# A new fixed order for the first batch of a packed-attention and two-MoE kernel, and keys by one transfer per four heads

## The chip, the cores and the metric

The kernel runs on one core of one Trainium2 chip. The metric is device time in microseconds (us) of one launch, the median of three runs. "PE" is TensorE, "DVE" VectorE, "ACT" ScalarE, "POOL" GpSimd and "SP" SyncE, whose queue starts nearly all transfers. A "product" below is one matmul instruction of the program; a product of plain fp32 operands shows as two MATMUL rows in the trace.

## The reference

```python
def sm_attn(qq, kk, vv):                      # per batch (8) and head (8); seq 576, head_dim 64
    s = scale * np.matmul(qq, kk.transpose(0, 1, 3, 2))
    s = s - np.max(s, axis=-1, keepdims=True)
    a = np.exp(s)
    a = a / (np.sum(a, axis=-1, keepdims=True) + 1e-09)
    return np.matmul(a, vv)
p_packed = sm_attn(p, k, v)                   # p: 32 packed queries per head
out = sm_attn(q, p_packed, p_packed)
x = out.transpose(0, 2, 1, 3).reshape(4608, 512)
x = gelu_like(x @ w_in) @ w_out               # w_in 512 x 2048, w_out 2048 x 512, given in float64
return (silu(x @ w_gate) * (x @ w_val)) @ w_out2
```

## The kernel before

**Two rounds.** Round one takes the eight batches in turn. Per batch it does the attention of two groups of four heads and the first MoE layer on the batch's 576 rows, in 32 units: two halves `t` of 288 rows, times 16 blocks `m` of 128 hidden columns. Round two does the gated layer; the change does not touch it.

**One unit.** `p1` (six products, tile `h`) multiplies `z`, the packed values already multiplied by `w_in`, with the second softmax `a2`. `tanh` (ACT) and `gate` (DVE, tile `g`) apply the activation. `hi` (ACT) and `lo` (POOL or DVE) split the result into a high and a low part, tile `gh`, so that three fast products stand for one of full precision. `p2` (twelve products, tile `acc`) multiplies by block `m` of `w_out`, tile `wo`. The tile `h` has two PSUM buffers, `gh` four.

**The attention of a batch**, per group `g`: `load_raw` brings keys or queries, `do_T` transposes them on DVE in two halves, `sc1` forms the scores of the packed queries (PE), `max1` (DVE), `exp1` (ACT) and `norm1` (DVE) make the first softmax. `a1T` transposes it on PE, `copy_a1T` copies it from PSUM, `pv` multiplies it with `v`. `do_D` copies 32x32 blocks of the result into `dz`; `do_F` (batch 0) or `do_E` and `split_E` (batch 1) put it into the form that `zm` multiplies with `w_in` (tile `zp`); `zh` and `zl` split that into `z`. `sc2`, `max2`, `exp2`, `norm2`, `ah` and `al` make the second softmax `a2`. All these take their PSUM buffers from one pool of two (`ps_a`).

**The weights in the first batch.** `w_in` and `w_out` arrive as float64 words. `stage` loads a block of 512 KB, `rebias` (ACT), `low` (ACT or DVE) and `join` (DVE) turn it into float32, `oh` and `ol` split a `w_out` block. `store_w n` writes two finished `w_in` blocks to DRAM (`win1`); in batch 1 `win`, `wch`, `wcl` and `wst` load, split and store them again (`win2`).

**What sets the order.** The string `FIRST` (line 19) is a list of these steps for batch 0, with the preparation of batch 1 marked by `+`. It is pinned: each engine gets its instructions in the order of the list, and each waits for what it needs. The list ends before `p1` of unit 32, the first of batch 1. From there on `STEADY` (line 79) holds, which the change leaves alone. Of the 32 units the list holds all `p1` and 29 `p2`, in both versions.

**Padding.** `warm n` (line 306) issues `n` products of a constant mask whose result nobody reads. The list of before holds twelve such steps, with 126 products.

**Keys.** `load_raw` (line 317) brings the queries of the first two batches with one transfer per group, in which each partition reads one run of 18 rows (4.6 KB). Keys come with four transfers, one per head, in runs of two rows:

```python
SP.dma_start(out=t[32 * h:32 * h + 32].rearrange("p (n r) d -> p n (r d)", r=2),
             in_=src[b, g * HG + h].rearrange("(n i r) d -> i n (r d)", i=32, r=2))
```

Of the kernel before, what the change touches and what calls it, by code (L numbers as in the profile page):

```python
# [20 lines left out]
    exp1 0; load_raw 1; warm 17; stage in 4; rebias in 4; do_T 1 0; do_T 1 1; stage in 1; pad_F 0; load_raw 2; do_T
    2 0; rebias in 0; sc1 1; warm 17; max1 1; low in 4 dve; join in 4; norm1 0; stage in 5; load_v 0 0; exp1 1;
    norm1 1; low in 0 act; stage in 7; rebias in 5; stage out 2; load_raw 3; a1T 0; copy_a1T 0; join in 0; pv 0;
    do_D 0 act; do_F 0; do_T 2 1; low in 7 dve; sc2 0 0; max2 0 0; low out 2 act; warm 9; rebias out 2; join out 2;
    do_T 3 0; rebias in 7; load_v 0 1; join in 7; a1T 1; copy_a1T 1; exp2 0 0; warm 5; stage in 6; low in 6 act; low
    in 5 dve; do_T 3 1; norm2 0 0; rebias in 6; pv 1; do_D 1 act; pad_F 1; do_F 1; warm 4; ah 0 0; stage out 0;
    stage out 13; join in 5; stage out 1; warm 6; low in 1 dve; stage in 3; oh 2; rebias in 1; al 0 0 dve; stage in
    9; join in 6; stage in 2; ol 2 pool; store_w 3; sc2 1 0; max2 1 0; exp2 1 0; low out 1 act; join in 1; zm 3; zm
    2; rebias out 0; store_w 2; norm2 1 0; rebias out 1; join out 1; ah 1 0; low out 0 act; al 1 0 pool; oh 1; ol 1
    pool; stage out 4; zh 3; zh 2; warm 27; zl 3 dve; zl 2 dve; store_w 0; join out 0; load_p 1; +do_p; low in 3  # L30
    dve; rebias out 4; zm 0; rebias in 3; rebias in 2; low in 2 dve; join in 2; join in 3; store_w 1; low out 13
    dve; zm 1; +p_ahead; zh 0; zl 0 dve; low out 4 act; p1 6; sc2 0 1; rebias out 13; stage in 8; rebias in 8; join
    out 4; zh 1; low in 8 dve; tanh 6; join out 13; stage out 8; zl 1 dve; p1 0; gate 6; rebias in 9; hi 6; stage in
    10; low in 9 act; stage in 11; stage out 5; tanh 0; rebias in 10; join in 8; max2 0 1; p1 2; tanh 2; warm 6;
    warm 5; gate 0; rebias in 11; join in 9; low in 11 dve; zm 4; lo 6 pool; oh 0; oh 13; sc2 1 1; p1 4; gate 2;
    join in 11; oh 4; stage in 15; low in 10 act; ol 0 dve; store_w 4; low out 5 act; exp2 0 1; ol 13 pool; ol 4
    pool; join in 10; max2 1 1; hi 0; lo 0 dve; low in 15 act; rebias in 15; hi 2; join in 15; zh 4; zl 4 dve; tanh
    4; rebias out 5; gate 4; zm 5; p1 1; lo 2 dve; join out 5; stage in 14; rebias in 14; zh 5; stage out 3; p1 3;
    p2 0; low out 3 dve; rebias out 3; join out 3; tanh 1; gate 1; stage out 10; hi 4; p1 5; zl 5 dve; low out 8
    act; lo 4 pool; rebias out 8; join out 8; stage in 13; p2 4; tanh 3; low in 14 dve; tanh 5; gate 3; oh 8; join  # L40
    in 14; zm 7; p1 8; stage in 12; low in 13 dve; rebias in 13; join in 13; rebias in 12; hi 1; lo 1 pool; low in
    12 dve; join in 12; zm 6; hi 3; stage out 12; load_raw 4; oh 5; ol 5 dve; p2 1; lo 3 dve; tanh 8; zh 7; oh 3;
    exp2 1 1; store_w 7; zh 6; zl 7 dve; low out 10 act; gate 8; rebias out 12; low out 12 act; hi 8; ol 3 pool; p2
    3; stage out 6; ol 8 pool; gate 5; hi 5; +do_T 0 0; +do_T 0 1; lo 8 pool; zl 6 dve; rebias out 10; stage out 9;
    p1 7; norm2 1 1; ah 1 1; al 1 1 pool; join out 10; low out 6 act; +sc1 0; +max1 0; p1 13; oh 10; ol 10 dve; tanh
    13; load_raw 5; +do_T 1 0; p2 8; +do_T 1 1; rebias out 6; load_v 1 0; tanh 7; join out 12; load_raw 6; join out
    6; +exp1 0; lo 5 pool; p2 5; +sc1 1; gate 13; oh 12; stage out 11; oh 6; gate 7; ol 12 pool; hi 13; low out 9
    act; store_w 6; +win 0; +max1 1; p1 11; +norm1 0; hi 7; p2 2; lo 13 dve; ol 6 pool; lo 7 pool; p2 6; +exp1 1;
    +norm1 1; store_w 5; rebias out 11; low out 11 act; join out 11; +a1T 0; wch 0; +copy_a1T 0; +do_T 2 0; +do_T 2
    1; oh 11; ol 11 pool; +win 2; tanh 11; stage out 7; gate 11; p1 10; tanh 10; wch 2; +pv 0; wcl 2 dve; p1 12; hi  # L50
    11; lo 11 dve; stage out 14; p2 13; +win 1; rebias out 9; gate 10; +do_D 0 act; +raw_ahead 0; wcl 0 pool; wst 0;
    rebias out 7; join out 9; hi 10; +do_E 0; low out 7 act; join out 7; lo 10 pool; +a1T 1; +split_E 0; p1 15; wch
    1; tanh 12; p2 11; +copy_a1T 1; +sc2 0 1; oh 7; wcl 1 pool; +zm 0 0; ol 7 dve; p2 7; gate 12; tanh 15; low out
    14 act; +win 4; gate 15; oh 9; +do_T 3 0; +zc 0 0; +max2 0 1; hi 15; lo 15 dve; p2 10; p1 14; +za 0 0; load_v 1
    1; tanh 14; p1 9; norm2 0 1; wch 4; ah 0 1; wcl 4 pool; +win 3; stage out 15; al 0 1 pool; gate 14; hi 14; tanh
    9; lo 14 pool; ol 9 pool; wst 1; +zm 0 1; +raw_ahead 2; +zc 0 1; +za 0 1; +pv 1; +do_D 1 act; +zh 0; wch 3;
    +do_E 1; wst 2; p1 17; +sc2 0 0; gate 9; hi 9; +zm 2 0; tanh 17; p1 21; rebias out 15; hi 12; lo 9 pool; +do_T 3
    1; +max2 0 0; rebias out 14; +sc2 1 1; wcl 3 dve; +zl 0 pool; lo 12 pool; gate 17; join out 14; +max2 1 1; +zc 2
    0; wst 4; oh 14; +za 2 0; +win 5; p2 9; low out 15 act; wst 3; hi 17; p1 16; +split_E 1; p2 12; wch 5; +zm 1 0;
    +exp2 0 1; ol 14 dve; +exp2 0 0; +win 6; wcl 5 dve; join out 15; +sc2 1 0; p2 14; tanh 21; gate 21; oh 15; lo 17  # L60
    dve; ol 15 pool; tanh 16; +win 7; p1 20; +zc 1 0; gate 16; hi 16; hi 21; lo 16 pool; wch 6; wst 5; +za 1 0; lo
    21 pool; +win 12; +raw_ahead 1; +norm2 0 1; p1 18; +zm 1 1; tanh 18; wch 7; gate 18; wcl 7 pool; p2 15; p2 16;
    +max2 1 0; wcl 6 pool; +zc 1 1; +za 1 1; tanh 20; gate 20; p1 26; +exp2 1 1; +norm2 1 1; tanh 26; hi 18; +zm 2
    1; wch 12; lo 18 pool; gate 26; wst 6; hi 20; p2 21; +win 9; +zc 2 1; +za 2 1; +zh 1; p1 19; tanh 19; +win 8; p2
# [1050 lines left out]
```

## Time and profile before

| | |
|---|---|
| median of 3 runs | 1662.6 us (1661.94 to 1662.65) |
| the profiled execution, its own time | 1662.05 us |
| its span, first to last instruction | 1660.2 us |
| PE busy, share of the span | 1635.6 us, 99% |
| DVE / ACT / POOL busy | 1133.4 / 766.1 / 281.2 us |
| mean granted TensorE clock | 0.997 of 2.4 GHz |

The span is 1.85 us shorter than the device time of the same execution. PE is counted as busy while a matmul is in its pipeline, so that 99% does not say that it ran at its peak, and padding counts as busy. What happens in the first batch is read from its own stretch of the trace and not from these totals.

### The profile page before, as it was taken

To read this page: it belongs to the slowest core of one execution; us is meant where nothing else is said; L and a number is where in the kernel's file an instruction comes from. 1 tells how busy PE (TensorE), PEld (TensorE's weight loads), DVE (VectorE), ACT (ScalarE), POOL (GpSimd) and SP (SyncE) were. 2 spreads that over 40 slices of the span, in tenths; PEclk is the share of its full clock that TensorE was granted. 3 is DMA by queue.
4 is the path that set the end of the run, shared out by engine and by line. 5 is a ranking of instruction groups with operands and counts; after the bars stand their busy time and mean duration, and the time that the engine had idled before them with its cause. 6 is when DMAs were issued, how large, how long until landed. Compare 5 with 4: busy or idle time off the path is not lost.

```text
span 1660.2 us, 26152 instructions
## 1 busy us (share of the span) xinstructions
PE 1635.6 (99%) x9468; PEld 1464.4 (88%) x9468; DVE 1133.4 (68%) x2133; ACT 766.1 (46%) x1646; POOL 281.2 (17%) x237
## 2 busy tenths in 40 slices
PE   8998999999999999999999999999999999999998
PEld 7788999999999999999988888888888888888887
DVE  5878777686977768686796465656567565846662
ACT  3776657566665656565653222332224222422222
POOL 0245023131312313021121110101010001000010
PEclk9999999999999999999999999999999999999999
DMA  8886757566574756345689454535444444525411
GB/s 269 280 256 211 210 181 227 160 219 186 167 240 121 229 150 216 130 142 167 206 317 324 141 166 140 164 93 184 146 152 134 149 156 139 159 77 178 140 50 51
DMA packets 173633, 291.67 MB, mean 176 GB/s; under 512 B 58816, under 2 KB 100800, under 8 KB 173504
## 3 DMA queue, kind: packets, MB, share of 16 engines
q1 hardware_dynamic: 171968, 285.27, 53.7%
q10 hardware_dynamic: 1536, 4.72, 0.8%
q8 instruction: 75, 1.23, 0.3%
q14 instruction: 54, 0.44, 0.1%
HBM read 227.02 MB, written 62.91 MB: 175 GB/s over the span
## 4 chain that ended last, share of the span: by engine, by line
PE 75%; DVE 11%; issue 4%; ACT 3%; DMA 2%; POOL 1%; SPq 0%; ACTq 0%; DVEq 0%; POOLq 0%
PE acc L151 32%; PE gv L151 30%; PE h L151 8%; DVE z L151 3%; PE sc L151 2%; DVE gh L151 2%; PE pv L151 2%; DVE g L151 2%; PE zp L151 1%; ACT z L151 1%; DVE x L151 1%; DVE T L151 1%; DVE sm L151 1%; DVE c L151 0%; DVE Th L151 0%
## 5 line engine op out<-in xcount | busy, mean ns | idle before, releaser
L151 PE MATMUL gv<-xh,w 128*128 128x512 f32 x2304 | 554.4, 389 | 0.0
L151 PEld LDWEIGHTS gv<-xh,w 128*128 128x128 f32 x2304 | 432.4, 188 | 89.7
L151 PE MATMUL acc<-gh,wo 128*128 128x288 f32 x3072 | 454.7, 296 | 1.7 <-POOL gh L151 0.9
L151 PEld LDWEIGHTS acc<-gh,wo 128*128 128x128 f32 x3072 | 426.7, 189 | 5.5 <-POOL gh L151 1.1
L151 PE MATMUL acc<-wo,gh 128*128 128x512 f32 x1296 | 326.8, 389 | 0.4
L151 PEld LDWEIGHTS acc<-wo,gh 128*128 128x128 f32 x1296 | 243.0, 188 | 52.1 <-DVE c L151 1.7
L151 PE MATMUL h<-a,z 128*128 128x288 f32 x1536 | 251.8, 299 | 3.4 <-DVE g L151 3.1
L151 DVE TENSOR_TENSOR gh<-g,gh 128x288 fp32r<-128x288 f32 (+1 forms) x285 | 172.1, 604 | 91.6 <-ACT gh L151 88.8
L151 PEld LDWEIGHTS h<-a,z 128*128 128x128 f32 x1536 | 221.0, 189 | 11.9 <-DVE g L151 4.6
L151 ACT CAST gh<-g 128x288 fp32r<-128x288 f32 (+1 forms) x304 | 139.9, 461 | 155.7 <-DVE g L151 106.9
L151 POOL TENSOR_TENSOR gh<-s,gh 128x512 fp32r<-128x512 f32 x60 | 82.3, 1371 | 699.1 <-ACT gh L151 655.4
L151 DVE TENSOR_TENSOR c<-gv,c 128x512 f32<-128x512 f32 x192 | 132.3, 689 | 84.0 <-ACT tb L151 56.6
L151 ACT CAST gh<-s 128x512 fp32r<-128x512 f32 x60 | 37.3, 621 | 248.7 <-DVE s L151 248.7
L151 DVE SCALAR_TENSOR_TENSOR g<-sig,h 128x288 f32<-128x288 f32 x256 | 113.8, 446 | 41.3 <-ACT sig L151 37.9
L151 ACT ACTIVATE sig<-h 128x288 f32<-128x288 f32 x256 | 104.1, 407 | 77.2 <-PE h L151 74.3
L151 DVE TENSOR_TENSOR ta<-gv,c 128x512 f32<-128x512 f32 x96 | 66.1, 689 | 83.4 <-PE gv L151 83.4
L151 POOL TENSOR_TENSOR z<-z,z 128x512 fp32r<-128x512 f32 x52 | 70.2, 1351 | 142.9 <-ACT z L151 142.8
L151 DVE TENSOR_TENSOR z<-zp,z 64x512 f32<-64x512 f32 (+1 forms) x120 | 81.9, 684 | 17.7 <-ACT z L151 14.5
L151 ACT ACTIVATE s<-c 128x512 f32<-128x512 f32 x48 | 30.3, 632 | 95.8 <-DVE c L151 95.8
L151 PE MATMUL zp<-wh,E 128*128 128x512 f32 x224 | 66.8, 403 | 4.7 <-DVE z L151 3.6
L151 ACT COPY z<-zp 64x512 f32<-64x512 f32 x112 | 65.1, 581 | 10.1 <-PE zp L151 7.0
L151 ACT ACTIVATE s<-ta 128x512 f32<-128x512 f32 x48 | 30.3, 632 | 68.8 <-DVE ta L151 68.8
(133 smaller groups left out, 1527.1 us busy)
## 6 DMA issues: line engine op xcount, KB each, us to landing
w<-w2s SPq DMA_DIRECT2D x144, 512.0 KB, 3.3
wh<-win SPq DMA_DIRECT2D x96, 512.0 KB, 4.2
w2s<-w SPq DMA_DIRECT2D x36, 512.0 KB, 3.8
...
```

The costliest lines, as they stand in the source:

```text
L151: x = getattr(self.engine, name)(*a, **k)
```

## The change

The list `FIRST` is replaced by another one. It holds the same steps but for the padding, which is five steps with 61 products (the change's own words speak of 61 in place of 268; the list of before adds up to 126). `store_w` is told which queue starts it: seven of the eight stores are now on SP's queue and one on ACT's; all eight were on ACT's. The copies of `do_D 0` of batch 1 move from ACT to DVE. In the first two batches keys come by one transfer per group, like the queries; a partition then holds 18 consecutive rows. `exp1` therefore writes its result with another stride, and `a1T` and `copy_a1T` divide the five blocks as 3 + 2 between two PSUM tiles in place of 4 + 1.

```diff
 FIRST = """
-    make_consts; warm 6; load_p 0; do_p; load_raw 0; do_T 0 0; stage in 0; warm 6; warm 18; do_T 0 1; sc1 0; max1 0;
...
+    stage in 3; rebias in 3; load_p 0; make_consts; do_p; low in 3 act; load_raw 1; do_T 1 0; warm 22; load_raw 0;
...
@@ load_raw
-        if b < 2 and j >= G:
+        if b < 2:
             SP.dma_start(out=t.rearrange("p n d -> p (n d)"),
                          in_=src[b, g * HG:g * HG + HG].rearrange("h (i n) d -> (h i) (n d)", i=32))
...
-    def store_w(n):
-        ACT.dma_start(out=win1[n], in_=wp[n])
+    def store_w(n, eng):
+        eng.dma_start(out=win1[n], in_=wp[n])
...
@@ exp1
             for t in range(2):
-                o = a[:, t * HK[0]:t * HK[0] + HK[t]].rearrange("p (n i r) -> p n r i", i=32, r=2)
-                ACT.activation(o, st["sc1", g][t][:, :HK[t]].rearrange("p (n r i) -> p n r i", i=32, r=2), AF.Exp,
-                               bias=st["mx1", g][:, 3:4], scale=SCALE, accum_out=s[:, t:t + 1])
+                x = st["sc1", g][t][:, :HK[t]]
+                if whole:
+                    o = a.rearrange("p (i n) -> p n i", n=NBLK)[:, t * HK[0] // 32:(t * HK[0] + HK[t]) // 32]
+                    x = x.rearrange("p (n i) -> p n i", i=32)
+                else:
+                    o = a[:, t * HK[0]:t * HK[0] + HK[t]].rearrange("p (n i r) -> p n r i", i=32, r=2)
+                    x = x.rearrange("p (n r i) -> p n r i", i=32, r=2)
+                ACT.activation(o, x, AF.Exp, bias=st["mx1", g][:, 3:4], scale=SCALE, accum_out=s[:, t:t + 1])
...
@@ a1T, copy_a1T
-            ps = [ps_a.tile([P, 4, P], F32, tag="a", name="a1T") for _ in range((NSC + 3) // 4)]
+            ps = [ps_a.tile([P, 4, P], F32, tag="a", name="a1T") for _ in range(2)]
             for c in range(NSC):
                 c0 = min(c * P, S - P)
-                PE.transpose(ps[c // 4][:, c % 4], st["a1", g][:, c0:c0 + P], ident)
+                PE.transpose(ps[c // 3][:, c % 3], st["a1", g][:, c0:c0 + P], ident)
...
-            ACT.copy(t[:, 0:2], ps[0][:, 0:2])
-            DVE.tensor_copy(t[:, 2:4], ps[0][:, 2:4])
-            ACT.copy(t[P - TAIL:, 4], ps[1][P - TAIL:, 0])
+            ACT.copy(t[:, :3], ps[0][:, :3])
+            DVE.tensor_copy(t[:, 3], ps[1][:, 0])
+            DVE.tensor_copy(t[P - TAIL:, 4], ps[1][P - TAIL:, 1])
```

PE, the opening of the program, before. `idle` is padding, `sc` the scores (from `Tp` and `pb` the first, from `T` and `dz` the second), `zp` the output of `zm`, `h` that of `p1`:

```order
L151 MATMUL a1T<-ident,a_166 128x128 x5
L151 MATMUL pv<-a1T,vt 128x128 x10
L151 MATMUL sc_302<-T,dz_92 128x288 x2
L151 MATMUL idle<-mask 128x128 x9
L151 MATMUL a1T<-ident,a_251 128x128 x5
L151 MATMUL idle<-mask 128x128 x5
L151 MATMUL pv<-a1T,vt 128x128 x10
L151 MATMUL idle<-mask 128x128 x10
L151 MATMUL sc_422<-Tp,dz_93 128x288 x2
L151 MATMUL zp<-wp,F_385 128x512 x2
L151 MATMUL zp<-wp,F_201 128x512 x2
L151 MATMUL idle<-mask 128x128 x27
```

The same place with the change, from the first `a1T` to the first `h`:

```order
L151 MATMUL a1T<-ident,a_178 128x128 x5
L151 MATMUL pv<-a1T,vt 128x128 x10
L151 MATMUL a1T<-ident,a_215 128x128 x5
L151 MATMUL sc_321<-T,dz_92 128x288 x2
L151 MATMUL sc_340<-T,dz_92 128x288 x2
L151 MATMUL pv<-a1T,vt 128x128 x10
L151 MATMUL idle<-mask 128x128 x5
L151 MATMUL sc_386<-Tp,dz_93 128x288 x2
L151 MATMUL zp<-wp,F_305 128x512 x2
L151 MATMUL sc_421<-Tp,dz_93 128x288 x2
L151 MATMUL zp<-wp,F_159 128x512 x4
L151 MATMUL idle<-mask 128x128 x8
```

Before, two more `zp` follow the last row and then the first `h`; now the first `h` follows at once. Ahead of the first `a1T` there were 30 + 17 + 17 padding products around the two first scores, and there are 22 + 13 + 13.

SP, its first rows before:

```order
L151 DMA pt<-in_p_dram 128x2x64
L151 DMA raw<-in_k_dram 32x9x128 x4
L151 DMA w64in_128<-in_moe_w_in_dram 128x1024
L151 DMA raw<-in_k_dram 32x9x128 x4
L151 DMA w64in_192<-in_moe_w_in_dram 128x1024
L151 DMA w64in_199<-in_moe_w_in_dram 128x1024
L151 DMA raw<-in_q_dram 128x1152
```

and with the change:

```order
L151 DMA w64in_95<-in_moe_w_in_dram 128x1024
L151 DMA pt<-in_p_dram 128x2x64
L151 DMA raw<-in_k_dram 128x1152 x2
L151 DMA w64out_152<-in_moe_w_out_dram 128x1024
L151 DMA w64in_161<-in_moe_w_in_dram 128x1024
L151 DMA w64in_175<-in_moe_w_in_dram 128x1024
L151 DMA raw<-in_q_dram 128x1152
```

Both keys now come as two transfers right behind one weight block; the second group's keys stand first.

SP a little further on with the change, where the first two stores of `win1` stand among the loads, with what each row waits for:

```order
L151 DMA w64in_326<-in_moe_w_in_dram 128x1024 [waits DMAHW3_49]
L151 DMA win_85<-wp 128x1024 [waits DMAHW4_49,DVE_49]
L151 DMA win_85<-wp 128x1024 [waits DMAHW5_49,DVE_49]
L151 DMA w64in_411<-in_moe_w_in_dram 128x1024 [waits DMAHW6_49]
L151 DMA w64in_413<-in_moe_w_in_dram 128x1024 [waits DMAHW7_49]
L151 DMA w64in_481<-in_moe_w_in_dram 128x1024 [waits DMAHW0_49]
L151 DMA w64out_495<-in_moe_w_out_dram 128x1024 [waits DMAHW1_49]
```

Each store waits for a `join` on DVE, and the loads behind it wait with it; before, these rows stood on ACT's queue.

## Rows read from the trace of the kernel before

**Rows 1.** The page, its first lines: span and busy time by engine

```profile
span 1660.2 us, 26152 instructions
...
PE 1635.6 (99%) x9468; PEld 1464.4 (88%) x9468; DVE 1133.4 (68%) x2133; ACT 766.1 (46%) x1646; POOL 281.2 (17%) x237
```

**Rows 2.** Busy time by stretch, to and from the first h product: us, engines, PEclk, DMA

```profile
0.00:53.30 53.30, 46.94 (x319) 41.05 (x320) 31.88 (x76) 22.23 (x57) 5.42 (x14) 1.00 0.83 256
53.30:173.40 120.10, 111.20 (x703) 99.83 (x701) 99.38 (x195) 87.99 (x202) 49.61 (x45) 0.97 0.79 253
```

**Rows 3.** Timeline of PE, opening: start us, us, engine line operation, count, idle before

```profile
1.65 9.32 PE L151 MATMUL idle<-mask 128*128 128x128 f32 x60 [1.65 <-DVE mask L151]
10.80 2.11 PE L151 MATMUL sc<-Tp,pb 128*128 128x320 f32 x8
12.74 3.96 PE L151 MATMUL idle<-mask 128*128 128x128 f32 x34
16.54 2.11 PE L151 MATMUL sc<-Tp,pb 128*128 128x320 f32 x8
...
22.28 0.71 PE L151 MATMUL a1T<-ident,a 128*128 128x128 f32 x5
...
29.49 2.17 PE L151 MATMUL idle<-mask 128*128 128x128 f32 x18
...
32.04 1.28 PE L151 MATMUL idle<-mask 128*128 128x128 f32 x10
...
35.39 2.40 PE L151 MATMUL idle<-mask 128*128 128x128 f32 x20
...
44.28 6.19 PE L151 MATMUL idle<-mask 128*128 128x128 f32 x54
...
53.34 1.39 PE L151 MATMUL h<-a,z 128*128 128x288 f32 x6
...
57.16 2.62 PE L151 MATMUL idle<-mask 128*128 128x128 f32 x22
59.62 1.88 PE L151 MATMUL zp<-wp,F 128*128 128x512 f32 x4
```

**Rows 4.** Timeline of SP's transfers, opening

```profile
1.30 1.95 SPq L151 DMA_DIRECT2D raw<-in_k_dram  x4
...
3.79 1.93 SPq L151 DMA_DIRECT2D raw<-in_k_dram  x4
```

**Rows 5.** Busy time by stretch of 1 us: last column is GB/s

```profile
2.00:3.00 1.00, 1.00 (x6) 1.00 (x6) 0.14 (x1) 0.08 (x1) 0.51 (x3) 1.00 0.72 181
...
14.00:15.00 1.00, 1.00 (x12) 1.00 (x11) 1.00 (x2) 1.00 (x5) 0.00 (x0) 1.00 1.06 427
```

**Rows 6.** Timeline of DVE, opening

```profile
6.89 1.44 DVE L151 STREAM_TRANSPOSE Tp<-raw 128x576 f32<-128x576 f32 x2 [2.99 <-DMA raw<-in_k_dram]
12.08 0.49 DVE L151 TENSOR_REDUCE mx<-sc 128x1 f32<-128x320 f32 x1 [3.75 <-PE sc L151]
...
13.78 1.44 DVE L151 STREAM_TRANSPOSE Tp<-raw 128x576 f32<-128x576 f32 x2
...
55.76 0.44 DVE L151 SCALAR_TENSOR_TENSOR g<-sig,h 128x288 f32<-128x288 f32 x1
```

**Rows 7.** Timeline of ACT, opening

```profile
13.79 0.56 ACT L151 ACTIVATE a<-sc,mx 128x320 f32<-128x320 f32 x1 [11.71 <-DVE mx L151]
...
26.22 1.50 ACT L151 COPY dz<-pv 32x32 f32<-32x32 f32 x8 [2.65 <-PE pv L151]
```

**Rows 8.** Timeline of PE, around the second stretch at half clock

```profile
149.26 0.70 PE L151 MATMUL zp<-wh,E 128*128 128x512 f32 x2 [2.98 <-DVE z L151]
...
151.09 2.79 PE L151 MATMUL acc<-gh,wo 128*128 128x288 f32 x12
...
155.45 1.78 PE L151 MATMUL acc<-gh,wo 128*128 128x288 f32 x12
```

**Rows 9.** Busy time by stretch of 1 us, inside and behind it: PEclk is third from the end

```profile
151.00:152.00 1.00, 1.00 (x6) 1.00 (x5) 1.00 (x3) 0.75 (x3) 0.95 (x1) 0.50 0.66 215
```

More of the change, by code (lines that the diff above doesn't have):

```diff
@@ L19 @@
 FIRST = """
-    make_consts; warm 6; load_p 0; do_p; load_raw 0; do_T 0 0; stage in 0; warm 6; warm 18; do_T 0 1; sc1 0; max1 0;
[L21 to L64, printed above, removed]
@@ L75 @@
-    +v_ahead 0; +za 5 1; p1 31; p2 28; gate 30; hi 30; lo 30 dve; +zh 5; wst 14; tanh 31; +zm 7 1; +zl 5 dve; +zc 7
-    1; +ah 0 0; p2 27; +za 7 1; +zh 7; +al 0 0 dve; +al 1 0 pool; wst 15; gate 31; +raw_ahead 3; +zl 7 dve
+    stage in 3; rebias in 3; load_p 0; make_consts; do_p; low in 3 act; load_raw 1; do_T 1 0; warm 22; load_raw 0;
+    do_T 0 0; do_T 0 1; stage out 0; rebias out 0; low out 0 dve; join out 0; pad_F 0; stage in 1; join in 3; sc1 0;
+    max1 0; stage in 4; do_T 1 1; exp1 0; rebias in 1; low in 1 act; norm1 0; load_raw 3; warm 13; sc1 1; max1 1;
@@ new lines @@
+    exp1 1; stage in 2; do_T 3 0; do_T 3 1; join in 1; load_v 0 0; warm 13; a1T 0; copy_a1T 0; load_raw 2; do_T 2 0;
+    rebias in 2; stage in 5; stage out 1; pv 0; stage in 0; do_D 0 act; load_v 0 1; stage out 6; norm1 1; low in 2
+    dve; join in 2; do_T 2 1; do_F 0; stage in 6; stage out 4; pad_F 1; low in 0 dve; a1T 1; copy_a1T 1; rebias in
+    0; join in 0; sc2 0 0; stage in 7; stage in 9; rebias out 1; oh 0; rebias in 4; rebias in 5; max2 0 0; sc2 0 1;
+    exp2 0 0; low in 4 act; low out 1 act; pv 1; max2 0 1; norm2 0 0; do_D 1 act; rebias out 6; warm 5; sc2 1 1;
@@ new lines @@
+    do_F 1; join in 4; join out 1; max2 1 1; low out 6 act; low in 5 act; join in 5; oh 1; store_w 0 sp; zm 1; zh 1;
+    store_w 2 sp; stage in 11; stage in 8; zl 1 dve; ah 0 0; al 0 0 pool; low in 6 act; sc2 1 0; max2 1 0; exp2 0 1;
+    exp2 1 0; join out 6; norm2 1 0; zm 0; exp2 1 1; zm 2; rebias in 6; join in 6; zh 0; low in 7 act; ah 1 0; al 1
+    0 pool; zl 0 dve; warm 8; p1 3; rebias in 9; norm2 0 1; stage in 12; rebias in 7; oh 6; zh 2; tanh 3; join in 7;
+    low in 9 act; gate 3; stage out 3; rebias in 8; p1 0; tanh 0; ol 6 dve; hi 3; gate 0; low in 8 act; join in 9;
@@ new lines @@
+    +do_T 1 1; p2 4; load_raw 6; p1 10; tanh 10; lo 8 pool; p2 5; join out 13; rebias out 12; oh 13; gate 10; tanh
+    14; hi 11; ol 10 dve; +sc1 1; stage out 8; low out 12 act; hi 10; +max1 1; low out 8 act; +raw_ahead 0; +norm1
+    0; rebias out 8; join out 8; p2 9; p1 12; tanh 12; lo 11 pool; gate 12; lo 10 pool; store_w 7 sp; +raw_ahead 3;
+    gate 14; p2 10; p1 16; p1 13; +do_T 2 0; ol 13 pool; join out 12; +exp1 1; oh 8; ol 8 dve; +a1T 0; +copy_a1T 0;
+    +norm1 1; p2 8; +win 0; +do_T 2 1; wch 0; wcl 0 dve; +do_T 3 0; hi 14; store_w 6 sp; oh 12; lo 14 pool; +win 1;
@@ new lines @@
+    stage out 14; hi 12; tanh 13; ol 12 dve; low out 15 act; store_w 5 act; lo 12 pool; tanh 16; +pv 0; +do_D 0 dve;
+    wch 1; wcl 1 pool; +do_E 0; p2 11; rebias out 15; gate 16; +split_E 0; load_v 1 1; +a1T 1; join out 15; rebias
+    out 14; +copy_a1T 1; low out 14 act; p2 12; join out 14; oh 14; ol 14 pool; gate 13; hi 13; lo 13 pool; +zm 0 0;
+    +zc 0 0; +za 0 0; +sc2 0 1; +max2 0 1; +do_T 3 1; hi 16; p1 15; tanh 15; +win 4; wst 0; +win 3; wch 4; wst 1; p1
+    18; tanh 18; +pv 1; gate 18; +exp2 0 1; oh 15; +do_D 1 act; p2 14; +v_ahead 1; lo 16 pool; +sc2 1 0; wcl 4 pool;
```

46 lines of the change are left out of this document (35 added, 11 removed).

## The prediction

> **What bounds the kernel now.** The change can move only what lies ahead of unit 32, the first unit of batch 1, so the question is when PE reaches that unit. The page [rows 1] has PE busy 99% of the span and is no guide here: padding counts as work. I read three views in this order.
>
> The timeline of PE's opening [rows 3] shows three stages. Up to the first `a1T` at 22.28 PE works through two score steps and 60 + 34 + 34 rows of padding. From there to the first `h` at 53.34 it has 18 + 10 + 20 + 54 rows of padding among its own work. The table by stretch [rows 2] then cuts at that first `h`. Ahead of it DVE is busy 31.88 of 53.30 us and DMA moves at a share of 0.83: nothing is full. Behind it, up to unit 32 at 173.4, DVE is busy 99.38 of 120.10 us (83%), ACT 87.99, DMA 0.79: four resources that are all nearly full, so that the stretch has little to give. The timelines of DVE and ACT [rows 6, 7] say what the opening waits for: DVE stood idle 2.99 us for keys and 3.75 us for scores, ACT 11.71 us for the first maximum and 2.65 us for the first `pv`. So the opening is a chain with padding in it, and the middle is a matter of load.
>
> **The keys.** The first group's keys were issued from 1.30 on and DVE could transpose them at 6.89; the second group's from 3.79, transposed at 13.78 [rows 4, 6]. While keys flow the transfers make 181 GB/s, while weights and queries flow 427 [rows 5]. In the new order one weight block (512 KB), `p` (64 KB) and both keys (576 KB each) stand ahead of everything else, 1.77 MB. From 2.2 on, at 410 GB/s, that takes 4.3 us, and 0.4 us to land: both keys are there by 6.9. The first group gains nothing; the second gains 7 us, of which the path sees only what padding leaves. "DMA: Bandwidth & Descriptors" of the Trainium skill, section Specifications, holds pieces of 512 B to be enough for full line rate; by it merging would not lift the rate, both keys at 181 GB/s would land at 10.5, the first score would start at 11.9 in place of the 8.4 below, and the sum would be 3.5 us smaller. The row above, 181 against 427, speaks against it. The keys of batch 1 I cost at nothing: they are wanted in the middle, where they lie beside other transfers; if that cover went, each would bring at most 576 KB at 181 less the same at 427, some 1.8 us.
>
> **Up to the first `a1T`.** Padding rows cost 9.15 / 60 = 0.153 us each in the first batch of them (1.65 to 10.80) and 3.80 / 34 = 0.112 later (12.74 to 16.54) [rows 3]. The new list has 44, 26 and 26. So: 1.65 + 44 x 0.153 = 8.4; the score step 1.9 (10.80 to 12.74), 10.3; 26 x 0.112 = 2.9, 13.2; the second step, 15.1; 2.9 again, 18.0. The dependencies fit under it: the keys with their two transposes (1.44, rows 6) are ready at 8.3; maximum, `exp1` and `norm1` of group 0 take some 4 us from 10.3; the maximum and `exp1` of group 1, whose PSUM buffers `a1T` needs, some 2 us from 15.1. So `a1T` starts at 18.0 and not 22.28: **-4.3 us**.
>
> **From there to the first `h`.** Before, it took 53.34 - 22.28 = 31.1 us. Padding was 102 x 0.112 = 11.4. PE's own work was two `a1T` (0.6 each), two `pv` (2.3), two `sc2` (0.75) and four `zm` (1.75, half of the 8 rows whose place is 3.5 us), 14.3 us in all. The remaining 5.4 us were waits, for `do_D` (1.50, rows 7) and joins above all. Now the list has 13 padding products, 26 rows, 2.9 us; four `sc2` and three `zm`, 14.0 us. If the waits stay at 5.4, the first `h` comes at 18.0 + 14.0 + 2.9 + 5.4 = 40.3. One check speaks for a little more. DVE has nearly the same work ahead of the first `gate` in either list, some 34 us (31.88 by 53.30, then on to 55.76, rows 2, 6); by 42 it would have to be busy 82% of the time, which is just what it reaches in the middle. I add 1 us: first `h` at 41.3, **-12.0 us** in all.
>
> **The middle.** The same steps remain: one `zm` more (+1.75), two `sc2` fewer (-1.5), and 22 rows of padding gone (57.16 to 59.62, 2.46 us). Those stood in front of PE while it had nothing else, so they may turn into waiting; bounds 0 and -2.46, and I take the whole, since units that are ready follow sooner. Taken as 120.10 + 0.2 - 2.5, unit 32 starts at 41.3 + 117.8 = 159.1 in place of 173.4. I assume that the new order wastes as much in the middle as the old, 120.10 - 99.38 = 20.7 us by DVE's account; this is the largest choice in the sum, and the bounds are all of it (-20.7) or as much again.
>
> **Small terms.** `exp1` writes with another stride; the trace has no such write. Bounds: the 0.56 us of rows 7, or twice that, four of them in the opening, 0 to +2.2; I take 0, since the old write was strided too. `copy_a1T` moves 64 rows' copy from ACT to DVE, and `do_D 0` of batch 1 eight small copies: 1.5 us of load between two engines that both have idle time (rows 2), 0. Seven `store_w` move from ACT's queue to SP's: at 0, as long as SP is ahead of its loads; without that cover see below.
>
> Sum: -12.0 - 2.5 + 0.2 = -14.3 us. The profiled execution took 1662.05 us, 0.6 below the median of the runs: 1662.05 - 14.3 = **1648**.
>
> **Rivals.**
> *The middle packs better.* All engines have work earlier, and the long queue of ready steps could fill half of DVE's 20.7 idle us: -14.3 - 10 = 1638. For it: the new list keeps more units open at once. Against it: ACT and DMA are loaded too.
> *PE's clock falls.* After 2.98 us of waiting PE ran at a granted clock of 0.50, the 1.2 GHz level [rows 8, 9], and twelve `acc` rows took 2.79 in place of 1.78 us. Such a stretch with its other work cost about 1.6 us, and before had two. With nearly half of the padding's time out of the opening (28.1 to 15.4 us) and all of it out of the middle, five more are thinkable, +8: 1656. Against it: padding remains in front of both scores, and waits of 1 to 2 us in the opening left the clock at 1.00 (rows 2). "TensorE: Matmul & The Clock Gate" of the Trainium skill, Part 1, says that the slow state is the default and activity lifts it, which is the reason for padding and speaks against taking it out; rows 8 agree that waiting brings the low level back.
> *The head start is absorbed*, because the `w_out` blocks that `p2` needs come no sooner: same time, 1661. The transfers up to 173.4 are 0.83 x 53.3 + 0.79 x 120.1 = 139 us of full DMA; that is below 159 by 20, so this needs holes.
> *Slower: SP's queue stands still behind stores.* A `store_w` on SP waits for a join on DVE, and every load behind it waits too. DMA's slack is the 20 us just named plus the 14 gained; divided by seven stores, from 5 us of standstill per store on the gain is gone. At 7 us each it would be 7 x 7 - 34 = +15: 1677. For it: two stores follow each other in the early queue with five loads behind them. Against it: most joins are done long before their store's turn, and eight transfers stay in flight.
> *The change does less than it says*: the list of before has 126 padding products, not 268, so 65 go and not 207. The sum counts rows and has that in it.
>
> **How the numbers follow.** Forecast 0.62 (its own range 1642 to 1655), better packing 0.14, low clock 0.09, absorbed 0.06, SP 0.09. 0.2%, 3.3 us, is about what a measurement of this kernel can tell. Faster by more: 0.62 + 0.14 + 0.09 = 0.85 less 0.02 for a low clock that takes nearly everything, 0.83; same 0.07; slower 0.10. The range reaches into better packing and past the low clock: 1636 to 1659.
>
> **What would show it.** Right: first `a1T` near 18, first `h` near 41, keys' transposes at 5 to 9 us, first `h` to unit 32 near 118 us with DVE above 80%, PEclk 1.00 in the opening. Wrong: the first `h` after 47; a middle of over 130 us; SP waiting at `win` rows with DMA's share low; stretches at 0.50 in the first 60 us; or a difference that arises behind unit 32.

## The result, and the profile after

The changed kernel took **1645.65 us** (median of 4 runs, 1643.6 to 1646.98) beside 1662.45 us of the kernel before on the same chip (1661.94 to 1662.65): a ratio of 0.9898, with a 95% interval of 0.9881 to 0.9915. The forecast was 1648, in a range of 1636 to 1659. The profiled execution took 1645.83 us, with a span of 1644.1.

The first lines of the page answer to [rows 1]: PE is busy 15.6 us less, the other engines about as much as before.

```profile
span 1644.1 us, 25884 instructions
...
PE 1620.0 (99%) x9338; PEld 1446.1 (88%) x9338; DVE 1140.5 (69%) x2157; ACT 766.1 (47%) x1626; POOL 277.5 (17%) x233
```

The table by stretch is cut where [rows 2] are cut, at the first `h` (42.2) and at unit 32 (154.9, before 173.4). Columns: stretch, PE, PEld, DVE, ACT, POOL, then PEclk, DMA share, GB/s.

```profile
0.00:42.20 42.20, 36.72 (x215) 30.03 (x216) 30.42 (x76) 24.02 (x57) 3.44 (x13) 1.00 0.91 299
42.20:154.90 112.70, 104.66 (x666) 91.66 (x665) 101.64 (x201) 85.48 (x191) 46.40 (x41) 1.00 0.86 281
```

Nearly the same DVE and ACT work now stands in less time. DVE's idle time falls from 21.4 to 11.8 us in the first stretch and from 20.7 to 11.1 in the second, and the transfers, at 256 and 253 GB/s before, run at 299 and 281. PE's granted clock is 1.00 in both; the second stretch of before had 0.97.

The timeline of PE's opening answers to [rows 3] (start us, us, engine line operation, count, idle before).

```profile
1.65 7.93 PE L151 MATMUL idle<-mask 128*128 128x128 f32 x44 [1.65 <-DVE mask L151]
9.76 2.33 PE L151 MATMUL sc<-Tp,pb 128*128 128x320 f32 x8 [0.17 <-DVE Tp L151]
11.92 3.06 PE L151 MATMUL idle<-mask 128*128 128x128 f32 x26
14.82 2.11 PE L151 MATMUL sc<-Tp,pb 128*128 128x320 f32 x8
16.76 3.06 PE L151 MATMUL idle<-mask 128*128 128x128 f32 x26
19.66 0.71 PE L151 MATMUL a1T<-ident,a 128*128 128x128 f32 x5
...
40.53 1.95 PE L151 MATMUL idle<-mask 128*128 128x128 f32 x16
42.23 1.87 PE L151 MATMUL h<-a,z 128*128 128x288 f32 x12
```

The first `a1T` comes 2.6 us earlier than before and the first `h` 11.1 us earlier. DVE's timeline answers to [rows 6]:

```profile
5.41 0.31 DVE L151 STREAM_TRANSPOSE pT<-pt 128x128 f32<-128x128 f32 x1 [3.48 <-DMA pt<-in_p_dram]
...
7.46 0.78 DVE L151 STREAM_TRANSPOSE Tp<-raw 128x576 f32<-128x576 f32 x1 [1.01 <-DMA raw<-in_k_dram]
8.92 1.44 DVE L151 STREAM_TRANSPOSE Tp<-raw 128x576 f32<-128x576 f32 x2 [0.69 <-DMA raw<-in_k_dram]
...
44.23 0.44 DVE L151 SCALAR_TENSOR_TENSOR g<-sig,h 128x288 f32<-128x288 f32 x1
```

And SP's to [rows 4]; each key group is now one transfer, and two stores stand among the early loads:

```profile
0.80 0.40 SPq L151 DMA_DIRECT2D w64in<-in_moe_w_in_dram  x1
1.26 0.42 SPq L151 DMA_DIRECT2D pt<-in_p_dram  x1
1.73 0.94 SPq L151 DMA_DIRECT2D raw<-in_k_dram  x2
...
28.63 8.02 SPq L151 DMA_DIRECT2D win<-wp  x2
36.71 1.76 SPq L151 DMA_DIRECT2D w64in<-in_moe_w_in_dram  x3
```

**Where the time came from.** The n-th `gate` row on DVE gives a clock for the whole batch. The new kernel leads by 11.6 us at the first (44.2 against 55.8), by 15.2 at the 9th (72.2, 87.4), 15.9 at the 25th (134.9, 150.8), 18.8 at the 32nd (155.3, 174.1) and 16.0 at the 256th (817.5, 833.5). So two thirds arise in the opening, the rest in the middle, and nothing behind unit 32, where 2.8 us of the lead go again.

To see what PE gave up, I added up all of its rows of the trace from the first `a1T` to the 32nd `gate`, in three kinds: its own products (a product counts from the end of the one before it, or from its start if that is later), padding, and waiting, which is the time in which no row ran. Some kernels of the next section stand beside the two.

| kernel | first `a1T` | first `h` | own products | padding | waiting | 32nd `gate` |
|---|---|---|---|---|---|---|
| before | 22.3 | 53.3 | 124.3 | 13.8 | 13.7 | 174.1 |
| before, half the padding | 20.4 | 52.6 | 126.8 | 8.9 | 16.4 | 172.5 |
| before, no padding | 20.4 | 55.8 | 134.5 | 0 | 20.6 | 175.6 |
| before, five steps moved | 21.7 | 50.5 | 124.6 | 13.8 | 14.3 | 174.5 |
| after | 19.7 | 42.2 | 121.0 | 2.9 | 11.8 | 155.3 |
| after, no padding | 20.1 | 41.8 | 121.6 | 0 | 12.8 | 154.5 |
| after, keys first, stores on ACT | 18.9 | 43.5 | 125.0 | 2.9 | 21.4 | 168.2 |

Padding and waiting together fall from 27.5 to 14.7 us, own products by 3.3, and the time ahead of `a1T` by 2.6, which is the whole 18.8 us. Whether the 11 us of padding in that were a cost or only the visible form of a wait is what the first experiments ask.

### The profile page after: what moved, and what is told of

It is laid out like the page before. It is cut to its first block, busy times and chain, and to the rows that moved or that the text cites. A ratio compares the mean times of both kernels' runs of the same rounds, so it can differ in the third digit from the quotient of the medians.

```text
span 1644.1 us, 25884 instructions
## 1 busy us (share of the span) xinstructions
PE 1620.0 (99%) x9338; PEld 1446.1 (88%) x9338; DVE 1140.5 (69%) x2157; ACT 766.1 (47%) x1626; POOL 277.5 (17%) x233
## 4 chain that ended last, share of the span: by engine, by line
PE 83%; DVE 6%; issue 4%; DMA 2%; ACT 1%; POOL 0%; DVEq 0%; SPq 0%; ACTq 0%; POOLq 0%
PE acc L151 36%; PE gv L151 30%; PE h L151 10%; PE sc L151 3%; PE zp L151 2%; PE pv L151 2%; DVE z L151 1%; DVE gh L151 1%; DVE g L151 1%; ACT z L151 1%; DMA wh<-win 1%; DVE c L151 0%; PE a1T L151 0%; DMA x<-x2d 0%; DMA w2s<-w 0%
## 5 line engine op out<-in xcount | busy, mean ns | idle before, releaser
L151 PEld LDWEIGHTS h<-a,z 128*128 128x128 f32 x1536 | 219.9, 188 | 12.4 <-DVE g L151 6.2
L151 ACT ACTIVATE s<-c 128x512 f32<-128x512 f32 x48 | 30.3, 632 | 95.9 <-DVE c L151 95.9
L151 ACT ACTIVATE s<-ta 128x512 f32<-128x512 f32 x48 | 30.3, 632 | 68.8 <-DVE ta L151 68.8
```

The source lines that it names most:

```text
L151: x = getattr(self.engine, name)(*a, **k)
```

## Experiments

All kernels ran beside the kernel before on their own chip (1663 to 1665 us there), so ratios are compared; the new kernel's is 0.9898. A trace shows one execution, and openings of the same list differ: in the four kernels with extra work further down, whose list is the new kernel's up to the first `a1T`, that came at 20.3 to 22.2 us in place of 19.7. In two of them, a_xact and a_xdma, PE was at the 1.2 GHz level for some 3 us between 11 and 16. So one or two microseconds between two openings say little.

### Padding

**b_nopad**: the old order without any `warm`; **a_nopad**: the new order likewise.

```diff
-make_consts; warm 6; load_p 0; ...; zh 2; warm 27; zl 3 dve; ...
+make_consts; load_p 0; ...; zh 2; zl 3 dve; ...
```

> The order of before with its twelve padding steps taken out (126 products), nothing else. Theory A, padding stood on the path: in the opening 60 + 34 + 34 and 102 rows go; the second score must still wait for the second keys (transposed by 15.2 us), so the first a1T comes at about 20 in place of 22.3, and the 11.4 us of padding behind it go for the most part, so the first h comes at 44 to 48 in place of 53.3 and the kernel takes 1653 to 1658 us. Theory B, padding only filled waits and held the clock: first h within 2 us of 53.3, the granted clock at 0.50 in stretches of the opening, 1662 us or more, up to 1672.

> The new order with its last five padding steps taken out (61 products). Theory A, padding costs where it stands in front of work: the two times 2.9 us around the second score go, less what the chain of maximum, exp1 and norm1 needs, so the first a1T comes 1 to 3 us sooner, 1643 to 1645 us if the clock holds. Theory B, this padding holds the clock: stretches at 0.50 in the first 45 us at 1.6 us or more each, 1647 to 1653 us.

Measured: b_nopad 1665.93 us, ratio 1.001 (1.0 to 1.0019); a_nopad 1645.96, ratio 0.989 (0.9876 to 0.9903). In the old order, 126 products less bring nothing. The table by stretch of b_nopad shows what takes their place:

```profile
15.20:25.40 10.20, 5.80 (x23) 4.62 (x22) 5.36 (x15) 2.81 (x8) 0.00 (x0) 0.50 1.02 293
25.40:28.80 3.40, 1.60 (x10) 0.95 (x8) 0.86 (x2) 2.34 (x10) 0.00 (x0) 1.00 1.03 244
28.80:49.30 20.50, 15.85 (x39) 9.68 (x39) 14.57 (x32) 10.30 (x26) 3.21 (x3) 0.50 0.60 238
```

Two stretches are at the lower clock, PE's own products take 10.2 us more, and it waits 7.0 us more (table above). In the new order almost nothing happens: the first `a1T` comes no sooner (20.1) although 96 padding rows ahead of it are gone, and from there to the first `h` it is 21.7 in place of 22.6, without the 2.9 us of padding; the clock fell once, from 21.2 to 24.7 us. Neither theory had that for the new order. With no padding in either list the two kernels lie 0.012 apart (1.001 against 0.989), some 20 us: the whole gain stands without padding having a part in it, though a little of the 20 may be what b_nopad's low clock costs.

**b_halfpads** takes half of each padding step ahead of the first `h` out of the old order, so that the clock keeps some cover.

```diff
-warm 6; ...; warm 18; ...; warm 17; ...; warm 17; ...; warm 9; ...; warm 27; ...
+warm 3; ...; warm 9; ...; warm 8; ...; warm 8; ...; warm 4; ...; warm 14; ...
```

> The old order and the old loads with every padding count up to the first product halved (110 products in place of 115 or more: of 219 about 109 go), so that PE's clock has half of its cover left. The prediction's step that padding is time on the path (0.112 to 0.153 us for each) says about 13 us less up to the first product and up to 13 us less at the end. The theory that padding stands in waits which end when they end: first product within 2 us of 53.3 and the end within 2 us, as long as the clock stays up; if it falls, as it did without any padding, PE's own products take the padding's place and the end is 0 to +3 later.

The counts in that text are muddled: 115 products stood there and 56 are left, 230 and 112 rows. At the prediction's prices the 118 rows are worth 30 x 0.153 + 88 x 0.112 = 14.4 us. Measured: 1662.95 us, ratio 0.9997 (0.9988 to 1.0006). PE's timeline:

```profile
9.08 1.95 PE L141 MATMUL idle<-mask 128*128 128x128 f32 x16
13.53 2.24 PE L141 MATMUL sc<-Tp,pb 128*128 128x320 f32 x8 [2.50 <-DVE Tp L141]
15.61 1.95 PE L141 MATMUL idle<-mask 128*128 128x128 f32 x16
20.42 0.74 PE L141 MATMUL a1T<-ident,a 128*128 128x128 f32 x5 [2.86 <-DVE sm L141]
...
40.88 3.67 PE L141 MATMUL zp<-wp,F 128*128 128x512 f32 x8 [2.53 <-DVE wp L141]
44.39 3.29 PE L141 MATMUL idle<-mask 128*128 128x128 f32 x28
47.51 1.95 PE L141 MATMUL zp<-wp,F 128*128 128x512 f32 x4
51.19 1.98 PE L141 MATMUL zp<-wp,F 128*128 128x512 f32 x4 [1.73 <-DVE wp L141]
52.61 1.35 PE L141 MATMUL h<-a,z 128*128 128x288 f32 x6
```

Where padding was shortened a wait for DVE stands in its place, before the second `sc`, before `a1T` and before the last `zp`. The first `zp` waits for the same `join` as in the kernel before and starts no sooner than there:

```profile
40.77 3.67 PE L151 MATMUL zp<-wp,F 128*128 128x512 f32 x8 [2.01 <-DVE wp L151]
```

The first `h` moved by 0.7 us. The clock did fall twice here (0.50 from 22.1 to 25.6 and from 29.0 to 32.4), and PE's own products took 2.5 us more; but the `zp` groups behind that waited for DVE all the same. So in the old opening padding stood in waits, and a padding row had next to no price.

### The keys

**b_newkeys**: the old order with each key group of the first two batches as one transfer (and the code that goes with it). **a_oldkeys**: the new order with four transfers per group and the old write of `exp1`.

```diff
-if b < 2:
+if b < 2 and j >= G:
     SP.dma_start(out=t.rearrange("p n d -> p (n d)"),
```

> The order of before, padding and all, with the keys of the first two batches by one transfer per group (and the exp1, a1T and copy_a1T that go with it). By my sum the keys alone give little, since padding stands in front of both scores: the second keys land some 3 us sooner, the opening moves by 0 to -1, total 1661 to 1663. Rival, the transfers were what held the opening: first h earlier by 3 us or more, 1659 or less. Rival, the new strided write of exp1 or the new division of a1T costs: first h later, 1664 or more.

> The new order with the four transfers per group of keys of before (and its exp1 write; a1T keeps the division 3 + 2). The keys stand on the path here, behind only 44 rows of padding: 2 x 576 KB at 181 in place of 400 GB/s land some 3.5 us later, so the first score and the first h come 3 to 4 us later; batch 1's keys add 0. 1648 to 1651 us. If the merged keys mattered nowhere: 1645.6 within 1. If they were the greater part of the gain: 1654 or more.

Measured: b_newkeys 1660.44 us, ratio 0.9976 (0.9965 to 0.9986); a_oldkeys 1648.43, ratio 0.9901 (0.9888 to 0.9915). In the old order the keys are worth 4 us (0.0024), a quarter of the change and more than the 0 to 1 us expected. By its trace only 0.9 us of that is there at the first `gate` (54.9) and 1.3 at the ninth (86.1); the rest comes later in batch 0, where the keys of batch 1 are loaded, which the prediction costed at nothing. The trace can't separate that from PE's clock, which fell at other places than before. In the new one the ratios of with and without, 0.9898 and 0.9901, can't be told apart; the traces have the first `a1T` at 23.4 instead of 19.7, the first `h` at 45.0 instead of 42.2 and the span at 1647.1 instead of 1644.1. Of that `a1T`, PE's 3.19 us wait for the last keys is the part that goes back to them (0.17 in the new kernel, 1.4 to 2.1 in the four others of the same opening); a stretch at the 1.2 GHz level, from 12.4 to 15.9 us, did much of the rest, as in a_xact. The rate is plain, in the four microseconds when keys flow: first a_oldkeys,

```profile
6.00:10.00 4.00, 2.69 (x25) 2.50 (x23) 1.43 (x2) 0.51 (x1) 0.00 (x0) 1.00 1.21 237
```

then the new kernel, ahead of it and during the keys:

```profile
2.00:5.00 3.00, 3.00 (x15) 3.00 (x15) 0.00 (x0) 0.09 (x1) 0.51 (x3) 1.00 0.80 236
5.00:9.00 4.00, 4.00 (x28) 4.00 (x27) 1.86 (x4) 1.23 (x2) 0.00 (x0) 1.00 1.02 409
```

The pieces of 512 B move at 237 GB/s while the DMA engines are full, the long rows at 409. The two differ in one thing more: a transfer of 512 B pieces goes to 32 partitions, one of long rows to 128.

**a_keysfirst** issues `p` and the keys ahead of the first weights.

```diff
-stage in 3; rebias in 3; load_p 0; make_consts; do_p; low in 3 act; load_raw 1; do_T 1 0; warm 22; load_raw 0;
+load_p 0; load_raw 1; load_raw 0; stage in 3; rebias in 3; make_consts; do_p; low in 3 act; do_T 1 0; warm 22;
```

> The new order with the load of p and the two key loads issued ahead of the first weights (in 3), whose 0.5 MB stood in front of them. If the keys bound the front: first key transposition 2 to 3 us earlier (about 5), first a1T 1.5 to 2.5 us earlier and the end 1 to 2 us below the new kernel. If the padding ahead of sc1 0 and the rebias and join of in 3 bound it: 0 to +1.

Measured: 1644.75 us, ratio 0.9891 (0.9876 to 0.9906). The keys landed at 5.38 and 7.16 in place of 7.43 and 8.90, the first `a1T` came at 18.8 (-0.9), the first `h` at 40.9 (-1.3), the 32nd `gate` at 154.6 (-0.7). That is half of what was expected, since the 44 rows of padding end at about 9 in any case, and too little for the medians to show, or for one trace to tell from another execution of the same opening.

### What the middle has to spare

Four kernels put extra work on one resource each, some 7 us of it (14 us on PE), spread over the units of batch 0 in the new order. a_xdve and a_xact repeat the `gate` or the `tanh` of every second unit, a_xpe puts `warm 4` ahead of every second `p1`, a_xdma stores four weight blocks a second time, to memory that nothing reads.

```diff
-        DVE.scalar_tensor_tensor(out=g, in0=s, scalar=1.0, in1=ps[:, :HS], op0=ALU.add, op1=ALU.mult)
+        for _ in range(2 if key[0] == 0 and key[2] % 2 == 0 and pin["on"] else 1):
+            DVE.scalar_tensor_tensor(out=g, in0=s, scalar=1.0, in1=ps[:, :HS], op0=ALU.add, op1=ALU.mult)
```

> The new order with the gate of every second product of batch 0 done twice on DVE: 16 more instructions of 443 ns, 7.1 us, spread over 44 to 155 us. The theory that DVE is what the stretch from the first gate to unit 32 now waits for (103.0 us busy of 114.3): +5 to +7 us against the new kernel. The rival that the stretch is held by several resources alike: +1.5 to +4. The rival that it is held by the transfers (DMA busy 0.85 of it): 0 to +1.5.

> The new order with the tanh of every second product of batch 0 done twice on ACT: 16 more instructions of 409 ns, 6.5 us, at the same places. If DVE holds the stretch: 0 to +2 (ACT has 28 us of idle time there). If several hold it alike: +1.5 to +4. If the transfers hold it: 0 to +1.

> The new order with four padding products ahead of every second p1 of batch 0: 64 products, some 7.6 us of PE time. The prediction's step that padding is time on the path says +5 to +7.6. The theory that padding stands in waits that are there anyway: 0 to +2.5, PE's idle time in the stretch being 8 us.

> The new order with four of the stores of the first weights done twice, the second time into memory that nothing reads: 2.1 MB more, about 7 us of all DMA engines at the 303 GB/s of the stretch. If the transfers hold the stretch: +4 to +8. If DVE holds it: 0 to +1.5. If several hold it alike: +1.5 to +4.

| kernel | ratio to before (95%) | first `h` to 32nd `gate` | against the new kernel's 113.1 |
|---|---|---|---|
| a_xdve | 0.9914 (0.99 to 0.9927) | 115.9 | +2.8 |
| a_xact | 0.9912 (0.9899 to 0.9926) | 116.3 | +3.2 |
| a_xpe | 0.9919 (0.9905 to 0.9932) | 118.6 | +5.5 |
| a_xdma | 0.9909 (0.9895 to 0.9922) | 114.3 | +1.2 |

The ends lie 2 to 3.5 us above the new kernel's, too close to be ranked, and the intervals overlap with its own (0.9881 to 0.9915). The stretch itself ranks them, though on one profile each: in a_nopad, a_keysfirst and a_oldkeys, which leave it as it is, it took 112.7, 113.8 and 114.2. So a_xdma's 1.2 is not clear of that spread, the less so as PE was at the 1.2 GHz level in it twice (52.4 to 55.9 and 137.8 to 141.2 us); a_xdve's 2.8 has one such stretch (50.9 to 54.4), a_xact's and a_xpe's have none. DVE, for which I had a theory, is not what holds it: 7.1 us more cost 2.8 at most. PE comes nearest. Its row of the stretch, 5.6 us longer than the new kernel's:

```profile
42.50:160.80 118.30, 115.83 (x793) 105.89 (x792) 99.74 (x202) 85.65 (x191) 48.53 (x42) 1.00 0.82 269
```

PE was busy 104.66 of 112.70 and is now busy 115.83 of 118.30. The 64 extra products took 14.3 us in PE's rows, twice the 7.6 expected, since each is two rows. Of these 5.5 us came onto the path; PE's waits fell from 8.1 to 2.7 us, and the rows of its own products from 105.0 to 102.0. Here, with few waits left, padding does cost; in the old opening it hardly did.

### The order itself

**b_fix** moves five steps of the old order: two DVE steps into its idle time ahead of the first `F`, and the first product with its `tanh` and `gate` ahead of the z products that it doesn't need.

```diff
-do_D 0 act; do_F 0; do_T 2 1; low in 7 dve; ...; rebias out 4; zm 0; rebias in 3; ...; low out 4 act; p1 6; ...; tanh 6; ...; gate 6; ...
+do_D 0 act; do_T 2 1; low in 7 dve; do_F 0; ...; rebias out 4; p1 6; zm 0; tanh 6; rebias in 3; ...; gate 6; low out 13 dve; ...
```

> The old order with five steps moved: do_T 2 1 and low in 7 go ahead of do_F 0 on DVE, into its idle time of 3.47 us there, and p1 6 with its tanh and gate goes ahead of the second pair of z products (zm 0, zm 1), for which it does not need to wait. If the order of DVE's and PE's own work is what the opening loses: first product 5 to 7 us earlier (about 47), unit 32 and the end 1 to 4 us earlier. If only the loads and the later steps count: first product earlier, the end within 0.7 us of the kernel before.

Measured: 1663.52 us, ratio 1.0 (0.9989 to 1.001). The first `h` came at 50.5, only 2.8 us earlier, and the first `gate` at 54.3, 1.5 earlier; from the ninth (89.2, before 87.4) on nothing was left. The lines of PE, ACT and DVE say why the edit was poor:

```profile
39.35 5.37 PE L141 MATMUL zp<-wp,F 128*128 128x512 f32 x8 [2.02 <-DVE wp L141]
44.55 6.19 PE L141 MATMUL idle<-mask 128*128 128x128 f32 x54
50.50 1.03 PE L141 MATMUL h<-a,z 128*128 128x288 f32 x6
45.20 1.29 DVE L141 TENSOR_TENSOR z<-zp,z 128x512 fp32r<-128x512 f32 x2 [1.62 <-ACT z L141]
```

```profile
51.56 0.41 ACT L141 ACTIVATE sig<-h 128x288 f32<-128x288 f32 x1 [5.33 <-PE h L141]
51.87 1.21 ACT L141 ACTIVATE wp<-w64in 128x512 f32<-128x512 f32 x2
```

```profile
53.12 1.29 DVE L141 SCALAR_TENSOR_TENSOR wp<-wp,wc 128x512 int32<-128x512 int32 x2 [4.41 <-ACT wp L141]
54.33 0.45 DVE L141 SCALAR_TENSOR_TENSOR g<-sig,h 128x288 f32<-128x288 f32 x1
```

The 27 products of padding still stood in front of the moved product: its `z` was done at 46.5, and PE began it at 50.5, without a wait. So a padding step that filled a wait can stand on the path, here for some 4 us, once the wait is moved away. PE also ran the `zp` products before it partly at the 1.2 GHz level (39.5 to 43.0 us; 5.37 us in place of 3.67). And I put the `tanh` on ACT ahead of two `rebias` steps, ACT stood 5.33 us for the product, and DVE 4.41 us for the `rebias`. What was won on PE was lost behind the moved step. The experiment does not show which of the old order's steps costs what, nor what an early first product could be worth; it shows that this lead of 2.8 us was gone by the ninth unit.

**a_kf_stact** is a_keysfirst with the seven stores that the new order issues on SP issued on ACT, as before.

```diff
-store_w 0 sp; zm 1; zh 1; store_w 2 sp; ...
+store_w 0 act; zm 1; zh 1; store_w 2 act; ...
```

> The kernel of a_keysfirst with the seven stores of the first weights that the new order issues on SP issued on ACT instead (store_w n act). On SP the first store stands in front of the next one until its weights are joined, and the loads behind it come as late. If SP's hold delays work: 1 to 3 us below a_keysfirst (ratio to the kernel before 0.987 to 0.988) and the first product no later. If the loads come early enough anyway, or the DMA engines are full in that stretch: within 0.7 us. If ACT is held by the stores in turn (it waits for the join before it can issue): 1 to 3 us above.

Measured: 1656.96 us, ratio 0.9963 (0.995 to 0.9977), some **12 us slower** than a_keysfirst's 0.9891 and outside everything expected. Its timeline of SP, to be held beside the new kernel's above:

```profile
27.55 2.72 SPq L140 DMA_DIRECT2D w64in<-in_moe_w_in_dram  x5
33.31 21.09 SPq L140 DMA_DIRECT2D w64out<-in_moe_w_out_dram  x4
54.45 1.81 SPq L140 DMA_DIRECT2D w64in<-in_moe_w_in_dram  x3
```

SP is no longer held by stores and has five weight blocks on their way by 30.3, where the store held three of them back. But the stores come later, for two reasons. ACT reaches the first one late: the `join` that it needs ended at 27.7 (27.03 + 0.69 on DVE), but other steps stand ahead of it in ACT's order, and it was issued at 34.53, where SP had issued it at 27.11 in a_keysfirst; it landed at 42.21 in place of 37.70. The second was issued at 36.40, not much behind the 34.98 of a_keysfirst, but now the loads that SP had held back were on their way: it took 9.35 us in place of 3.82 and landed at 45.75 in place of 38.81. The third was issued at 53.67 in place of 38.57. The first weights have three buffers (`NWH`), and one is free only when its store has landed. ACT fills them, and waits for each:

```profile
34.53 0.38 ACTq L140 DMA_DIRECT2D win<-wp  x1
36.40 0.33 ACTq L140 DMA_DIRECT2D win<-wp  x1
42.29 0.66 ACT L140 ACTIVATE wp<-w64in 128x512 f32<-128x512 f32 x1 [3.09 <-DMA win<-wp]
45.82 1.24 ACT L140 ACTIVATE wp<-w64in 128x512 f32<-128x512 f32 x2 [1.51 <-issue]
53.67 0.33 ACTq L140 DMA_DIRECT2D win<-wp  x1
59.91 0.66 ACT L140 ACTIVATE wp<-w64in 128x512 f32<-128x512 f32 x1 [5.54 <-DMA w64in<-in_moe_w_in_dram]
66.87 0.66 ACT L140 ACTIVATE wp<-w64in 128x512 f32<-128x512 f32 x1 [4.11 <-DMA win<-wp]
```

The row at 59.91 names a load, but no load of `w_in` landed between 41.5 and 61.2 us, and the third store landed at 59.88; likewise the second at 45.75. So the four waits, 14.2 us in all, are waits for stores; in a_keysfirst ACT waits only once ahead of such a row in this stretch, 0.95 us for a load.

SP stands too (its row at 33.31 above lasts 21.09 us): 9.6 us until a load of its own has landed, then 7.8 for ACT, and from 44 to 52 the transfers run dry, at a share of 0.06. The stretches from 44 to 52 and from 37 to 60 here, then the latter in the new kernel:

```profile
44.00:52.00 8.00, 6.78 (x27) 4.79 (x26) 6.27 (x13) 6.49 (x14) 1.72 (x2) 0.79 0.06 26
37.00:60.00 23.00, 17.17 (x74) 11.67 (x74) 15.04 (x31) 12.55 (x28) 4.33 (x4) 0.93 0.61 219
```

```profile
37.00:60.00 23.00, 20.47 (x116) 16.16 (x117) 21.62 (x44) 19.27 (x42) 7.73 (x7) 1.00 0.91 308
```

DMA falls from 0.91 to 0.61, DVE from 21.62 to 15.04 us, and the ninth `gate` comes at 82.7 in place of 70.5. So the new order depends on the queue of its seven stores: issued on SP they leave as soon as their data are joined, and they keep the loads behind them from getting ahead of them, so that the three buffers turn over in time. How much is due to each, no run separates; stores on ACT but further ahead in its order were not tried. Nor are the 12 us a gain that could be taken over to the old order: the new list is arranged around stores on SP, and whether the old one would profit was not tried.

## Why the prediction was right, and where its steps were not

**The sum** was -14.3 us; the profiled execution fell by 16.2 (1662.05 to 1645.83). Direction, place and size held. Several terms under it did not, and that the size came out so near is partly luck: the middle gave 5.1 us more than forecast, the opening 0.9 less, and 2.3 of the lead at unit 32 (18.5 us) were lost behind it, where nothing was forecast. The sum credited 4.2, 8.5 and 2.5 us to padding that goes, more than the whole of it, and the runs give padding next to no part.

**The keys.** "At 410 GB/s" was right for the time when they flow (409). "From 2.2 on" was not: from 2 to 5 us 236 GB/s moved, so that the weight block and `p` in front landed at 5.15 and 5.39 and the keys at 7.43 and 8.90, not by 6.9. The Trainium skill, "DMA: Bandwidth & Descriptors", section Specifications, holds pieces of 512 B to be enough for full line rate. a_oldkeys decides against that for these transfers, with its 237 GB/s. The rate was higher with long rows, as the prediction had it, but in the new order the ratios show no gain by it.

**First `a1T`**, 18.0 forecast, 19.66 measured, -2.6 and not -4.3. The first padding rows took 7.93 / 44 = 0.180 us each where 0.153 was used (+1.2), the later ones 0.118 for 0.112, and the score then still waited 0.17 for the transposed keys: padding and keys ended together. In the four other profiles of this opening the score waited 1.4 to 2.1 us for the keys, and `a1T` came at 20.3 to 22.2: the keys, put at 8.3 with their transposes, were the later of the two.

**From `a1T` to the first `h`**, 23.3 forecast, 22.6 measured. The items of the new list were right: padding 2.9 as forecast, own products 16.2 for 14.0, waits 3.7 for 6.4 (the 5.4 and the 1 us added). But the step that carried it, that 11.4 us of padding become 2.9 while "the waits stay at 5.4", is **wrong as a cause**. In b_halfpads 118 rows went, 14.4 us by that price, and the first `h` moved 0.7. Padding in the old list filled waits. It was right by sum, and by luck as far as the price goes: the new order had less to wait for, and its list had been given less padding. The count of padding followed how long PE had to wait in each order, and the prediction read a symptom as a price. Had the change been the padding alone, the same step would have promised some 30 us (16.9, 11.4 and 2.5 of padding in PE's rows) for b_nopad, which gained none.

**The middle**, 117.8 forecast, 112.7 measured, is the term that was most mis-sized. That the new order "wastes as much in the middle as the old", 20.7 us by DVE's account, was called the largest choice, and it was off: 112.70 - 101.64 = 11.1 us, about the half that the rival of better packing named. Of the 7.7 us from first `h` to 32nd `gate`, PE's rows have 2.5 as padding, 3.5 as the `acc` products (48.7 to 45.2), which in the old kernel ran partly at the 1.2 GHz level [rows 8, 9], and 0.9 as waits; the rest lies in other products. The credit for 2.46 us of padding there may be partly right, as a_xpe has two fifths of such products on the path; b_nopad, without them, took 119.8 from first `h` to 32nd `gate` where the kernel before took 120.8. The clock seems to account for about 1.9 of the 3.5: in b_fix, which ran its middle at 1.00 (50.5 to 174.0), the `acc` products took 46.8.

**Small terms.** `store_w` on SP "at 0, as long as SP is ahead of its loads" is **wrong**: undone in the new list, it costs 12 us. The rest (`exp1`'s stride, `copy_a1T`, `do_D`) was not tried by itself.

**The rivals.** *SP stands still behind stores*: it did, from 29.35 to 36.3 in one stretch, 7.0 us and more than the 5 us named. The price was taken from DMA's slack, as though what is held back were lost. DMA was not idle meanwhile (0.94 of 28 to 37 us), because the five loads issued ahead of it were still under way, the last until 36.2, and what was held back were loads that, let go in a_kf_stact, lay in front of the second store. The mechanism was seen and its sign was not. *The clock falls*: in the profiled execution the granted clock is 1.00 all the way to unit 32. That was not so in each: a_xact, a_xdma and a_oldkeys were at 0.50 for some 3 us between 11 and 16, a_keysfirst from 133.1 to 136.6. But the four executions of the new kernel have a mean granted clock of 0.998 to 1.000 over the whole run, where five more such stretches of some 3 us would have made it about 0.995; so they did not come. The Trainium skill, "TensorE: Matmul & The Clock Gate", Part 1, says that the slow state is the default and activity lifts it. The trace of b_nopad agrees, whose opening without padding was at the low level for 30 us; a_nopad, whose PE waited 12.8 us where b_nopad's waited 20.6, was there from 21.2 to 24.7 only. *The head start is absorbed*: it was not, 11.6 us at the first `gate` grew to 16.0 at the last. But b_fix shows how a head start of the first product alone can be lost. *Better packing*: in the middle DVE's idle time did halve, as it said; with 2.3 us more of DVE work there (101.64 for 99.38) the stretch came out 5.1 us below the forecast, half of the rival's 10.

What stays open: which of the moved steps bring what; the runs show what is not the cause (padding) and what the new list can't do without (the stores on SP), but no run takes the old order to the new one step by step. Putting the old order's middle behind the new opening was not tried on the chip.
